# Slot experts reordered: layer one of all experts first, weights fetched in another order, one direct block instead of two

## The chip, the cores and the metric

The kernel runs on one core of a Trainium2 chip. The metric is the device time of one execution in microseconds (us), lower is better. Five queues of instructions run beside each other on the core: TensorE (PE in the rows; matmuls, and PEld for the loads of their stationary operand), VectorE (DVE), ScalarE (ACT), GpSimd (POOL) and SyncE (SP), which here only issues transfers (DMA).

## The reference

Three parts follow each other; the change touches the end of the second and the start of the third.

```python
# 1: attention with decay, 4 batches x 8 heads, 576 positions, head size 64 -> x of (2304, 512)
# 2: soft mixture of 8 experts with 4 slots each
logits = x @ phi                                  # (2304, 32)
d = softmax(logits, axis=0); slot_input = (d.T @ x).reshape(8, 4, 512)
for e in range(8):                                # "slot experts"
    h = np.maximum(slot_input[e] @ w1[e], 0.0)    # layer one: 512 -> 1024
    slot_out[e] = h @ w2[e]                       # layer two: 1024 -> 512
x = softmax(logits, axis=1) @ slot_out.reshape(32, 512)
# 3: dense mixture of 4 experts
for e in range(4):
    h = np.maximum(x @ m1[e], 0.0)                # m1: 512 x 1024
    out += p[:, e:e + 1] * (h @ m2[e])            # m2: 1024 x 512
```

## The kernel before, in words

**Weights.** All expert weights come as tiles of 128 x 1024 floats (512 KB), four for a layer of an expert, through `load_w` (L60), which takes the next one of the list `stream` and issues it on SP's queue. The order of the list is w1 and w2 of expert 0, of expert 1, and so on, then m1 and m2 of the dense experts. Tiles go, in this order, into `ring` (one buffer of four tiles), `ringb` (29 buffers), three pairs that take the place of attention's operands (`load_pair`), five tiles in `post`, issued when attention's buffers are free, and four in `post2`, issued when the tail of the slot soft-max is through with its space. That makes 48 tiles. The rest is loaded into buffers that the slot experts release (the dictionary `later`): w1 of expert six into `ring`, then w2 of six, w1 and w2 of seven and m1 of dense expert 0 into `ringb`, and m2 of dense expert 0 into `ring` as the last.

**Slot experts** (L746 to L830 and the first half of the block behind L948). `layer1(e)` multiplies all 32 slots with w1 of expert e: 32 matmuls with 32 stationary columns and 256 moving ones, four of them side by side in the array, into a PSUM bank; ScalarE takes the positive part. `turn(e)` transposes the result in two matmuls, GpSimd clears the tile `ht`, and VectorE copies the four slots that belong to the expert into it. `layer2(e)` is 16 matmuls of 512 moving columns, which add up in `so_ps` over all experts. TensorE runs layer one of the next expert between turn and layer two. A helper `c4_rep` on GpSimd makes replicas of the combine weights, which TensorE transposes (`c4_tr`) and ScalarE copies (`c4_hi`). `g_make` multiplies the slot outputs with m1, `g_spread` brings that into the layout of the gates `gs`, and `pieces` makes the hidden layer of a block of 256 rows: four matmuls for each half.

**Dense part.** Four experts x nine blocks of 256 rows. A *direct* block multiplies the hidden layer's quarters with the four quarters B00, B10, B01, B11 of m2, each split in a high (rounded) and a low part (`w_hi` on ScalarE, `w_lo` on VectorE or GpSimd): 8 products, 96 matmuls of 256 columns. Any other block needs 7 products, 84 matmuls, with sums T1 to T4 of the quarters (`w_sum`, GpSimd, 128 x 512 at a time), also split in two parts, and sums S1 to S4 of the hidden layer. Low parts of S1 to S4 are made by GpSimd in the block itself (L922). Before, the first two blocks are direct (`ND = 2`), and the quarters and sums of dense expert 0 are split while these run (`PRE0`). TensorE also makes the pieces of the block behind in each block (8 matmuls).

**Order.** Where `manual_schedule` names an engine, its instructions stand in program order; elsewhere a planner orders them. Before, the slot experts name TensorE only, the passage to the dense part names TensorE, ScalarE and VectorE, and the dense part all four. SP's queue is ordered by the planner. A pool of buffers that is opened over the space of closed ones waits for the instructions that use those.

Of the kernel before, what the change touches and what calls it, by code (L numbers as in the profile page):

```python
# [19 lines left out]
DM = H * D  # L20
# [14 lines left out]
def soft_moe_kernel(tc, a, out):  # L35
# [10 lines left out]
    NB = 29  # L46
    ND = 2
    with ExitStack() as top:
# [3 lines left out]
        ringb = attn.enter_context(tc.tile_pool(name="ringb", bufs=NB))  # L52
# [10 lines left out]
        def load_w(pl, n=1):  # L63
            for _ in range(n):
                kind, e, p = stream.pop(0)
# [7 lines left out]
        def load_ring():  # L73
            t = ring.tile([128, 4096], F32, tag="w", name=f"ring_{len(stream)}")
            for i in range(4):
                load_w(t[:, 1024 * i:1024 * i + 1024])
            return t
# [42 lines left out]
        def load_q(pr, r=slice(0, 128)):  # L120
            t = ringb.tile([128, 1024], F32, tag="w", name="q_1")[:, 0:S] if pr == 1 else raw[:, 0]
            sp.dma_start(out=t[r], in_=a["q"][pr, r])
            q_raw[pr] = t
# [26 lines left out]
        si_t = tl.tile([128, DC, 32], F32, name="si_t")  # L150
# [12 lines left out]
        pool.memset(mm[:, 0:1], -1e30)  # L163

# [343 lines left out]
        pre = ["ring"] * 4 + [ringb] * NB  # L508
        rt = []
        order = ExitStack()  # L510
        for g in range(NG + 4):
            pr, st = divmod(g, NS)
            if g < NG:
# [18 lines left out]
                if pre and g >= GW and g % PS == PO:  # L532
                    pl = pre.pop(0)
                    if pl == "ring":
                        if not rt:
                            rt.append(ring.tile([128, 4096], F32, tag="w", name="ring_0"))
                        pl = rt[0][:, 4096 - 1024 * (len(pre) - NB + 1):4096 - 1024 * (len(pre) - NB)]
# [13 lines left out]
        load_w(ex.enter_context(tc.tile_pool(name="post", bufs=5)), 5)  # L551
# [13 lines left out]
        with tc.manual_schedule(engines={E.PE, E.Activation, E.DVE}):  # L565
# [89 lines left out]
            for h in range(2):  # L655
                c = slice(2 * h, 2 * h + 2)
                dve.tensor_tensor(si_t[:, c], so[:, c], si_ps[h], op=ALU.add)
# [22 lines left out]
        def c4_rep(b):  # L680
            src = cn[:64, :, 4] if b == B else cn[:, b, 0:4]
            r = src.shape[0]
            c4 = c4p.tile([r, 4, 4, 32], F32, tag="c4f" if b == B else "c4", bufs=1 if b == B else 2, name=f"c4_{b}")
            chi = c4p.tile([r, 4, 32], F32R, tag="chi", name=f"chi_{b}")
# [60 lines left out]
        hrs = {}  # L745

        def layer1(e):
            t = ops.tile([128, DM], F32, tag="o", name="first") if e == 1 else bank(1, e % 2)
            w1 = wt["w1", e]
            for c in range(DC):  # L750
                for jq in range(4):
                    pe.matmul(t[32 * jq:32 * jq + 32, 0:256], lhsT=si_t[:, c, :],
                              rhs=w1[c][:, 256 * jq:256 * jq + 256], start=c == 0, stop=c == DC - 1)
            t = t[:, 0:256]
            hrs[e] = eo.tile([128, 256], F32, tag="hr", name=f"hr_{e}")
            act.activation(hrs[e], t, AF.Relu)

        hts = {}

        def turn(e):  # L760
            t = bank(0, e % 2)
            t = t[:, 0:256].rearrange("p (i q) -> p i q", i=2)
            for i in range(2):
                pe.transpose(t[:, i, :], hrs[e][:, 128 * i:128 * i + 128], ident)
# [26 lines left out]
        raws[0] = None  # L791
        later = {0: (ring, 4), 1: (ringb, 8), 2: (ringb, len(stream) - 44), 3: (ringb, 4), 5: (ring, 4)}
        layer1(0)
        for e in range(E1 - 2):
            with tc.manual_schedule(engines={E.PE}):
                if e == 0:
                    layer1(1)
                    turn(0)
                    layer1(2)
                    layer2(0)  # L800
                elif e == 1:
                    turn(1)
                    layer2(1)
                else:
                    turn(e)
                    layer1(e + 1)
                    layer2(e)
            if e in later:
                if later[e][0] is ring:
                    raws[0] = load_ring()  # L810
                else:
                    load_w(*later[e])
            if e == 5:
                ex.close()
                wsp = [top.enter_context(tc.tile_pool(name="wspa", bufs=1, side="right"))]
                c4tp = top.enter_context(tc.tile_pool(name="c4tp", bufs=1, side="right"))
                c4t = c4tp.tile([128, NT], F32R, name="c4t")
                so_t = c4tp.tile([128, DC, 32], F32, name="so_t")
                dpn = c4tp.tile([128, 18, E2], F32, name="dpn")
                sel = c4tp.tile([128, 4, 2, 128], F32R, name="sel")  # L820
                dpr = c4tp.tile([128, 18, E2], F32, name="dpr")
                dps = c4tp.tile([128, 18], F32, name="dps")
                sp.dma_start(out=dpr, in_=a["dp"])
                gsp = top.enter_context(tc.tile_pool(name="gsp", bufs=2, side="right"))
                cq = ExitStack()
                c4p = cq.enter_context(tc.tile_pool(name="c4p", bufs=1, side="right"))
                pool.memset(f32(sel), 0.0)
                for jq in range(4):
                    for i in range(2):
                        r = slice(32 * jq, 32 * jq + 32)  # L830
                        pool.tensor_scalar(sel[r, jq, i, 64 * i:64 * i + 64].rearrange("p (a s) -> p a s", a=2),
                                           i4[r, None, :].to_broadcast([32, 2, 32]), 1.0, 1.0, op0=ALU.mult,
                                           op1=ALU.mult)
                for b in (B, 0, 1):
                    c4_rep(b)
# [107 lines left out]
        with tc.manual_schedule(engines={E.PE, E.Activation, E.DVE}):  # L943
            turn(E1 - 2)
            layer1(E1 - 1)
            layer2(E1 - 2)
            turn(E1 - 1)
            c4_tr(B, c4_bank(B))  # L948
            c4_tr(0, c4_bank(0))
            for h in range(2):  # L950
                act.copy(orow[h], so_ps[:, 256 * h:256 * h + 256])
            free += [0, 1, 2, 3]
            c4_hi(B)
            c4_hi(0)
            for h in range(2):
                layer2_last(h)
            w_hi(0, "B00", act, 0, 2)
            c4_rep(2)
            for h in range(2):
                t = (bank(1, 1) if h == 0 else c4_bank("so"))[:, 0:64].rearrange("p (c s) -> p c s", c=2)  # L960
                for c in range(2):
                    pe.matmul(t[:, c, :], lhsT=orow[h][:, 128 * c:128 * c + 128], rhs=i4)
                dve.tensor_copy(so_t[:, 2 * h:2 * h + 2], t)
                if h == 0:
                    c4_tr(1, c4_bank(1))
                    c4_hi(1)
            c4_rep(3)
            w_lo(0, "B00", pool, 0, 2)
            w_hi(0, "B00", act, 2, 4)
            g_make(0, bank(0, 0)[:, 0:256], range(2))  # L970
            gg = g_make(0, bank(0, 0)[:, 0:256], range(2, DC))
            c4_tr(2, c4_bank(2))
            c4_hi(2)
            c4_tr(3, c4_bank(3))
            c4_hi(3)
            cq.close()
            attn.close()
            accp = top.enter_context(tc.tile_pool(name="accp", bufs=1))
            wsp.append(top.enter_context(tc.tile_pool(name="wspb", bufs=1)))
            top.enter_context(tc.tile_pool(name="skew", bufs=1)).tile([128, 24], F32, name="skew")  # L980
            hp = top.enter_context(tc.tile_pool(name="hp", bufs=1))
            ttp = top.enter_context(tc.tile_pool(name="ttp", bufs=1))
            free += [4, 5, 6, 7]
            for hf in range(2):
                g_spread(0, *gg, hf)
            pieces(0, 0)
            hi_d(0, 0, 0)
            lo_d(0, 0, 0)
            w_hi(0, "B10", act, 0, 2)
            w_lo(0, "B10", pool, 0, 2)  # L990
            hi_d(0, 0, 1)
            lo_d(0, 0, 1)
            pieces(0, 1)
            hi_d(0, 1, 0)
            lo_d(0, 1, 0)
            w_lo(0, "B00", dve, 2, 4)
            w_hi(0, "B10", act, 2, 4)
            w_lo(0, "B10", pool, 2, 4)
# [261 lines left out]
```

## Time and profile before

| | |
|---|---|
| median of 3 runs | 660.17 us (660.02 to 660.5) |
| profiled execution | 661.34 us, of it 659.5 in the span of the trace |
| TensorE busy | 649.1 us (98%) |
| VectorE, ScalarE, GpSimd busy | 486.6 (74%), 349.1 (53%), 417.3 (63%) |
| moved by DMA | 76.15 MB |

Attention runs to 201, the tail of the slot soft-max to 210, the slot experts to 244, the passage to 251, the dense part from there to the end. A busy share is an average over these stages; what ends last is read in each stage by itself. Times in rows are from the start of the span.

### The profile page before, as it was taken

The page shows a single profiled execution, that of the slowest core. Times are in us where ns is not written, and L with a number is a line of the kernel's source. Part 1 is how long each engine was busy: PE and PEld are TensorE (multiplying, and loading weights), DVE is VectorE, ACT ScalarE, POOL GpSimd, SP SyncE. Part 2 cuts the span into 40 slices and gives each one's busy share as a digit, 9 for nine tenths or more (in the row PEclk, how much of TensorE's full clock was granted, in tenths as well). Part 3 has the DMA queues.
Part 4 walks back from the last instruction along what each step waited for, and adds up shares of the span by engine and source line. Part 5 has one row for each costly group of instructions (what it writes and reads, how often), then busy time and mean ns, then how long its engine had stood idle before and what let it go on. Part 6 is the DMA issues. An engine that isn't in the chain of part 4 may idle for free.

```text
span 659.5 us, 15363 instructions
## 1 busy us (share of the span) xinstructions
PE 649.1 (98%) x5670; PEld 579.9 (88%) x5670; DVE 486.6 (74%) x1322; ACT 349.1 (53%) x844; POOL 417.3 (63%) x398
## 2 busy tenths in 40 slices
PE   8999999999999999999999999999999999999998
PEld 4778788788787448999999999999999999999997
DVE  6889889888884017777678877678877768876774
ACT  6777877777772025633457433538343446444441
POOL 5677777777641068833989653789753689844443
PEclk9999999999999999999999999999999999999999
DMA  5687687775347990303000303000303000011111
GB/s 170 192 241 224 210 263 225 221 247 167 86 167 268 411 419 27 127 3 128 1 1 1 129 1 129 1 1 1 129 1 129 2 1 1 33 49 49 58 40 65
DMA packets 27509, 76.15 MB, mean 115 GB/s; under 512 B 4014, under 2 KB 4654, under 8 KB 27436
## 3 DMA queue, kind: packets, MB, share of 16 engines
q1 hardware_dynamic: 27436, 75.18, 33.8%
q8 instruction: 45, 0.74, 0.5%
q14 instruction: 28, 0.23, 0.1%
HBM read 70.31 MB, written 4.72 MB: 114 GB/s over the span
## 4 chain that ended last, share of the span: by engine, by line
PE 86%; DMA 4%; DVE 3%; ACT 3%; issue 2%; POOL 0%; ACTq 0%; DVEq 0%
PE R L1049 27%; PE Q L1049 13%; PE P L1049 7%; PE avb L283 5%; PE pt L266 5%; PE two L856 5%; PE d L1069 3%; PE sc L233 3%; PE sc L217 3%; PE sc L230 3%; PE pl L335 2%; PE ava L295 2%; PE pt L257 2%; DMA w<-in_w 2%; DMA ring<-in_m 1%
## 5 line engine op out<-in xcount | busy, mean ns | idle before, releaser
L922 POOL TENSOR_TENSOR s<-S,s 128x512 fp32r<-128x512 f32 x136 | 174.8, 1317 | 134.4 <-ACT s L918 134.4
L918 ACT CAST s<-S 128x512 fp32r<-128x512 f32 x136 | 75.0, 619 | 86.0 <-PE Q L1049 49.5
L207 ACT ACTIVATE p<-p,nm 128x256 f32<-128x256 f32 (+2 forms) x144 | 83.4, 579 | 28.8 <-DVE nm L203 27.5
L1049 PE MATMUL R<-wh_T,s 128*128 128x256 f32 x544 | 86.5, 280 | 0.7 <-DVE acc L1032 0.7
L1032 DVE SCALAR_TENSOR_TENSOR acc<-R,dpn,acc 128x256 f32<-128x256 f32 x115 | 55.5, 482 | 36.8 <-PE R L1049 33.6
L888 ACT ACTIVATE a<-two 128x256 f32<-128x256 f32 x68 | 26.0, 383 | 96.4 <-PE two L856 96.0
L1049 PEld LDWEIGHTS R<-wh_T,s 128*128 128x128 f32 x544 | 73.6, 188 | 1.5 <-ACT a L897 1.3
L203 DVE CUSTOM_DVE_ANT_0 p<-sc,maskb 128x256 f32<-128x256 f32 (+2 forms) x144 | 66.9, 489 | 3.3 <-PE sc L217 1.1
L914 DVE SCALAR_TENSOR_TENSOR S<-two,S 128x256 f32<-128x256 f32 x136 | 57.1, 420 | 3.3 <-POOL s L922 0.5
L914 DVE SCALAR_TENSOR_TENSOR S<-two,a 128x256 f32<-128x256 f32 x136 | 56.4, 414 | 0.0
L184 POOL TENSOR_TENSOR opd<-raw,opd 64x576 fp32r<-64x576 f32 x29 | 42.4, 1461 | 14.0 <-ACT opd L169 12.9
L266 PE MATMUL pt<-ident,p 128*128 128x128 f32 x285 | 45.9, 279 | 1.3 <-ACT p L207 0.7
L856 PE MATMUL two<-c4t,gs 128*128 128x256 f32 x288 | 46.2, 283 | 0.9 <-ACT gs L169 0.9
L230 PE MATMUL sc<-opd 128*128 128x256 f32 (+3 forms) x128 | 46.5, 374 | 0.0
L904 DVE SCALAR_TENSOR_TENSOR q<-two,q 128x512 fp32r<-128x512 f32 x68 | 46.3, 681 | 0.0
L266 PEld LDWEIGHTS pt<-ident,p 128*128 128x128 f32 x285 | 31.4, 140 | 14.6 <-issue 10.2
L1049 PE MATMUL R<-wh_T,q 128*128 128x256 f32 x272 | 43.6, 282 | 0.0
L192 POOL TENSOR_TENSOR opd<-raw,opd 64x576 fp32r<-64x576 f32 x30 | 42.3, 1409 | 1.4
L1049 PE MATMUL R<-wh_B,a 128*128 128x256 f32 x272 | 43.0, 280 | 0.0
L1049 PE MATMUL P<-wh_B,q 128*128 128x256 f32 x272 | 43.0, 279 | 0.0
L1049 PE MATMUL Q<-wh_T,s 128*128 128x256 f32 x272 | 43.0, 280 | 0.0
L1049 PE MATMUL Q<-wh_B,s 128*128 128x256 f32 x272 | 43.0, 280 | 0.0
(272 smaller groups left out, 1658.0 us busy)
## 6 DMA issues: line engine op xcount, KB each, us to landing
w<-in_w SPq DMA_DIRECT2D x50, 512.0 KB
ring<-in_m SPq DMA_DIRECT2D x28, 512.0 KB
raw<-in_k SPq DMA_DIRECT2D x64, 144.0 KB
v<-in_v SPq DMA_DIRECT2D x16, 320.0 KB
out<-acc SPq DMA_DIRECT2D x17, 256.0 KB
ring<-in_w SPq DMA_DIRECT2D x8, 512.0 KB
raw<-in_q SPq DMA_DIRECT2D x28, 144.0 KB
w_opd<-in_w SPq DMA_DIRECT2D x4, 512.0 KB
```

What stands on the lines that cost most here:

```text
L184: (dve if h == 0 else pool).tensor_tensor(lo, r, f32(hi), op=ALU.subtract)
L203: dve.tensor_tensor_reduce(out=pt_in[j][:, k0:k0 + n], in0=sc, in1=maskb[:, m0:m0 + n], scale=-SCALE, scalar=nm, op0=ALU.add, op1=ALU.min, ...
L207: act.activation(p, p, AF.Exp, bias=nm, scale=-1.0, accum_out=sums)
L230: pe.matmul(o, lhsT=qa[hh][:, qs], rhs=ka[hh][:, 0:n], start=True, stop=False)
L266: pe.transpose(t[:, i, :], pt_in[j][:, 128 * i:128 * i + 128], ident)
L856: pe.matmul(t[:, j, k], lhsT=gs[e][:, 128 * fc:128 * fc + 128], rhs=c4t[:, nb * BLK:nb * BLK + BLK])
L904: dve.scalar_tensor_tensor(o[:, 1], i, 0.0, f32(o[:, 0]), op0=ALU.max, op1=ALU.subtract)
L914: dve.scalar_tensor_tensor(sv[m, name][:, c], half[m, h][:, :, k, 128 * t:128 * t + 128], 0.0, other, op0=ALU.max, op1=op)
L918: act.copy(tile_of(m, name)[:, 0], sv[m, name])
L922: (eng or pool).tensor_tensor(o[:, 1], sv[m, name], f32(o[:, 0]), op=ALU.subtract)
L1032: dve.scalar_tensor_tensor(o, t, pcol, o, op0=ALU.mult, op1=ALU.add)
L1049: pe.matmul(t, lhsT=a[:, c, :], rhs=w[:, c, :], start=first and x == 0 and c == 0, stop=x == 2 and c == 3, skip_group_check=True)
```

## The change

- `stream` lists w1 of all experts, then w2 of all, then m1 and m2. `ringb` becomes two pools of 17 and 14 buffers, the second of which is given up early (`brief`); `post` takes six tiles. 51 tiles are fetched ahead. The first four behind them are m2 of dense expert 0, into `ring`; then the last 13 of w2, then m1 of dense expert 0.
- The slot inputs lie in `si_f`, with 28 zero columns about the four of an expert, so that `layer1` of four experts adds up in one bank. ScalarE and `turn` run once for four experts; `slots(e)` makes an expert's `ht` with one multiply by a mask (`own`) on VectorE, in place of GpSimd's memset and the copy.
- The order is layer one of all eight, then layer two of all eight, with all four engines in program order from there to the end.
- Copies, sums and low parts of m2's quarters are placed among the last slot experts, and T1 and T2 get space there; one direct block is left (`ND = 1`), and `PRE0` holds only the rest.
- The scratch for dynamic DMA goes from its default size to 1024 bytes, and three memsets stand at the start.

```diff
-    NB = 29
-    ND = 2
+    NB = (17, 14)
+    ND = 1
...
-        ringb = attn.enter_context(tc.tile_pool(name="ringb", bufs=NB))
+        ringb = [attn.enter_context(tc.tile_pool(name="ringb", bufs=NB[0]))]
+        brief = ExitStack()
+        ringb.append(brief.enter_context(tc.tile_pool(name="ringc", bufs=NB[1])))
...
-        stream = [(kind, e, p) for e in range(E1) for kind in ("w1", "w2") for p in range(4)]
+        stream = [(kind, e, p) for kind in ("w1", "w2") for e in range(E1) for p in range(4)]
...
+        pool.memset(own, 0.0)
+        pool.memset(own.rearrange("p (e x) -> p e x", x=36)[:, :, 0:4], 1.0)
+        pool.memset(si_f, 0.0)
...
-        pre = ["ring"] * 4 + [ringb] * NB
+        pre = ["ring"] * 4 + [ringb[0]] * NB[0] + [ringb[1]] * NB[1]
...
-        load_w(ex.enter_context(tc.tile_pool(name="post", bufs=5)), 5)
+        load_w(ex.enter_context(tc.tile_pool(name="post", bufs=6)), 6)
...
         def layer1(e):
-            t = ops.tile([128, DM], F32, tag="o", name="first") if e == 1 else bank(1, e % 2)
+            t = l1[e // 4]
             w1 = wt["w1", e]
             for c in range(DC):
+                o = 128 * e + 32 * c
                 for jq in range(4):
...
+                    pe.matmul(t[32 * jq:32 * jq + 32, :], lhsT=si_f[:, o:o + 32],
+                              rhs=w1[c][:, 256 * jq:256 * jq + 256], start=e % 4 == 0 and c == 0,
+                              stop=e % 4 == 3 and c == DC - 1)
...
+        def slots(e):
             ht = eo.tile([128, 2, 4, 32], F32, tag="ht", name=f"ht_{e}")
-            pool.memset(ht, 0.0)
-            dve.tensor_copy(ht[:, :, :, 4 * e:4 * e + 4],
-                            t.rearrange("p a (j s) -> p a j s", j=4)[:, :, :, 4 * e:4 * e + 4])
+            dve.tensor_tensor(ht, tr1[e // 4],
+                              own[:, None, None, 32 * e:32 * e + 32].to_broadcast([128, 2, 4, 32]), op=ALU.mult)
...
+        man.enter_context(tc.manual_schedule(engines={E.PE, E.Activation, E.DVE, E.Pool}))
+        for e in range(E1):
+            if e == 4:
+                hidden(0)
+            layer1(e)
+            if e == 0:
+                raws[0] = load_ring(stream.index(("m2", 0, 0)))
+            elif e < 6:
+                load_w(ringb[0], 4 if e < 5 else 1)
+            if e == 4:
+                turn(0)
+                slots(0)
+                slots(1)
+        hidden(1)
+        for e in range(5):
+            layer2(e)
+            if e == 0:
+                turn(1)
+            if e < 3:
+                slots(e + 2)
+        ex.close()
+        brief.close()
...
+        for x in ("T1", "T2"):
+            w_sum(0, x, 0, 2)
+            w_sum(0, x, 2, 4)
+        pool.memset(f32(sel), 0.0)
...
+        w_hi(0, "B00", act)
+        w_hi(0, "B10", act)
+        w_lo(0, "B00", dve, 0, 2)
+        slots(5)
+        layer2(5)
+        w_hi(0, "B01", act)
+        w_hi(0, "B11", act)
+        w_hi(0, "T2", act)
+        w_hi(0, "T1", act)
+        for b in (0, 1, 2, 3, B):
+            c4_rep(b)
+        w_lo(0, "B00", dve, 2, 4)
+        slots(6)
+        w_lo(0, "B10", dve, 0, 2)
+        slots(7)
+        w_lo(0, "B10", dve, 2, 4)
...
+        g_make(0, bank(0, 0)[:, 0:256], range(2))
+        gg = g_make(0, bank(0, 0)[:, 0:256], range(2, DC))
+        for b in (1, 2):
+            c4_tr(b, c4_bank(b))
+            c4_hi(b)
+        for x in ("B01", "B11"):
+            w_lo(0, x, pool, 0, 2)
+            w_lo(0, x, pool, 2, 4)
+        for x in ("T3", "T4"):
+            w_sum(0, x, 0, 2)
+            w_sum(0, x, 2, 4)
...
+        PRE0 = {(0, 0): [("lo", "T2", "p", 0, 2)], (0, 1): [("hi", "T3", "a", 0, 4), ("lo", "T2", "p", 2, 4)],
+                (0, 2): [("hi", "T4", "a", 0, 4), ("lo", "T1", "p", 0, 2)], (0, 3): [("lo", "T1", "p", 2, 4)],
+                (0, 4): [("lo", "T3", "p", 0, 2)], (0, 5): [("lo", "T3", "p", 2, 4)],
+                (0, 6): [("lo", "T4", "p", 0, 2)], (1, 0): [("lo", "T4", "p", 2, 4)]}
...
-    nc = bacc.Bacc("TRN2", target_bir_lowering=False, num_devices=1)
+    nc = bacc.Bacc("TRN2", target_bir_lowering=False, num_devices=1, dynamic_dma_scratch_size=1024)
```

## Rows read from the trace of the kernel before

**Rows 1.** The chain that ended last, 224 to 262: start, length, what.

```profile
224.68 0.37 PE two L764 x2
225.05 1.86 PE two L752 x32
226.92 1.72 PE so_ps L776 x16
...
238.64 8.15 DMA ring<-in_m
```

**Rows 2.** Busy time of each engine by stretch, granted clock, DMA share, GB/s.

```profile
160.00:170.00 10.00, 10.00 (x94) 7.75 (x94) 8.67 (x35) 7.95 (x26) 7.96 (x9) 1.00 0.28 76
...
209.00:212.00 3.00, 2.94 (x40) 2.17 (x44) 1.25 (x7) 0.14 (x1) 1.02 (x3) 1.00 0.02 5
...
214.00:246.00 32.00, 31.65 (x396) 14.44 (x396) 2.83 (x12) 4.31 (x11) 11.31 (x30) 1.00 1.02 414
...
248.00:250.00 2.00, 1.16 (x8) 0.96 (x8) 0.69 (x1) 2.00 (x5) 1.89 (x2) 1.00 0.25 89
...
656.40:659.50 3.10, 0.00 (x0) 0.00 (x0) 0.46 (x1) 0.00 (x0) 0.00 (x0) 0.93 0.32 118
```

**Rows 3.** SP's timeline, 209 to 243: first issue, time to the last, what, count.

```profile
211.09 1.75 SPq L71 DMA_DIRECT2D w<-in_w  x4
...
212.93 1.89 SPq L71 DMA_DIRECT2D ring<-in_w  x4
214.92 15.32 SPq L71 DMA_DIRECT2D w<-in_w  x12
231.32 4.00 SPq L71 DMA_DIRECT2D m<-in_m  x4
236.21 3.97 SPq L71 DMA_DIRECT2D ring<-in_m  x4
```

**Rows 4.** Waits of SP's queue, 150 to 260: total, times, longest.

```profile
SPq L71 <- POOL cn L660: 1.1, 1, 1.1
```

**Rows 5.** Timeline of TensorE and ScalarE, 209 to 278 (idle before, releaser).

```profile
210.48 1.93 PE L752 MATMUL two<-ring,si_t 128*32 128x256 f32 x32
...
245.01 1.93 PE L928 MATMUL two<-m,so_t 128*32 128x256 f32 x32
...
246.79 0.62 ACT L737 CAST wh_B<-ring 128x512 fp32r<-128x512 f32 x1 [4.34 <-DMA ring<-in_m]
...
246.88 1.09 PE L694 MATMUL ct<-ident,c 128*128 128x128 f32 x8
...
247.88 0.62 ACT L737 CAST wh_B<-ring 128x512 fp32r<-128x512 f32 x1
...
251.50 0.39 PE L1069 MATMUL d<-wh_B,q 128*128 128x256 f32 x1 [0.21 <-ACT q L863]
...
276.88 0.63 PE L1049 MATMUL R<-wh_B,a 128*128 128x256 f32 x4
```

**Rows 6.** The chain in the dense part: a stretch of direct matmuls, two starts of blocks.

```profile
271.39 5.66 PE d L1069 x48
...
580.13 2.12 PE R L1049 x18
...
590.95 2.12 PE R L1049 x18
```

**Rows 7.** Groups by shape: count, busy us, mean ns of one, idle before.

```profile
L724 POOL TENSOR_TENSOR T<-ring 128x512 f32<-128x512 f32 x8 | 10.3, 1306 | 2.1 <-DMA ring<-in_m 2.1
...
L737 ACT CAST wh_B<-ring 128x1024 fp32r<-128x1024 f32 x9 | 9.4, 1049 | 0.0
...
L743 DVE TENSOR_TENSOR wl_B<-ring,wh_B 128x512 fp32r<-128x512 f32 x3 | 4.6, 1549 | 0.0
```

**Rows 8.** GpSimd's timeline: at the start, and the selector's memset.

```profile
4.91 0.77 POOL L182 TENSOR_SCALAR opd<-raw 64x576 fp32r<-64x576 f32 x1 [1.42 <-DMA raw<-in_q]
...
232.91 0.95 POOL L827 MEMSET sel<- 128x1024 f32 x1
```

More of the change, by code (lines that the diff above doesn't have):

```diff
@@ L120, in load_q @@
         def load_q(pr, r=slice(0, 128)):
[L121 removed]
+            t = ringb[1].tile([128, 1024], F32, tag="w", name="q_1")[:, 0:S] if pr == 1 else raw[:, 0]
             sp.dma_start(out=t[r], in_=a["q"][pr, r])
@@ L149, in soft_moe_kernel @@
         s_sb = tl.tile([128, DM], F32, name="s_sb")
-        si_t = tl.tile([128, DC, 32], F32, name="si_t")
+        si_f = tl.tile([128, E1 * 132], F32, name="si_f")
+        own = tl.tile([128, E1 * 36], F32, name="own")
+        si_t = si_f.rearrange("p (e x) -> p e x", x=132)[:, :, 0:128].rearrange("p e (c y) -> p e c y", y=32)[:, :, :, 0:4]
         mm = tl.tile([128, 5], F32, name="mm")
@@ L743, in w_lo, with hidden, turn @@
             eng.tensor_tensor(lo[:, c0:c1], source(e, name)[:, c0:c1], f32(hi[:, c0:c1]), op=ALU.subtract)
[L745 removed]
+        hrs, tr1, hts = {}, {}, {}
         def layer1(e):
[L748 removed]
+            t = l1[e // 4]
             w1 = wt["w1", e]
             for c in range(DC):
+                o = 128 * e + 32 * c
                 for jq in range(4):
[L752 to L762, printed above, removed]
+                    pe.matmul(t[32 * jq:32 * jq + 32, :], lhsT=si_f[:, o:o + 32],
+                              rhs=w1[c][:, 256 * jq:256 * jq + 256], start=e % 4 == 0 and c == 0,
+                              stop=e % 4 == 3 and c == DC - 1)
+        def hidden(g):
+            hrs[g] = eo.tile([128, 256], F32, tag="hr", name=f"hr_{g}")
+            act.activation(hrs[g], l1[g], AF.Relu)
+        def turn(g):
+            t = bank(g, 0)[:, 0:256].rearrange("p (i q) -> p i q", i=2)
             for i in range(2):
[L764 removed]
+                pe.transpose(t[:, i, :], hrs[g][:, 128 * i:128 * i + 128], ident)
+            tr1[g] = t.rearrange("p a (j s) -> p a j s", j=4)
+        def slots(e):
             ht = eo.tile([128, 2, 4, 32], F32, tag="ht", name=f"ht_{e}")
[L766 to L768 removed]
+            dve.tensor_tensor(ht, tr1[e // 4],
+                              own[:, None, None, 32 * e:32 * e + 32].to_broadcast([128, 2, 4, 32]), op=ALU.mult)
             hts[e] = ht
@@ L790, in soft_moe_kernel @@
         so_ps = ops.tile([128, DM], F32, tag="o", name="so_ps")
[L791 to L835, printed above, removed]
@@ new lines, in soft_moe_kernel @@
+        l1 = [bank(1, 0)[:, 0:256], ops.tile([128, DM], F32, tag="o", name="first")[:, 0:256]]
+        man = ExitStack()
+        man.enter_context(tc.manual_schedule(engines={E.PE, E.Activation, E.DVE, E.Pool}))
[11 more added lines that the diff above has]
+                slots(1)
@@ new lines, in soft_moe_kernel @@
+        hidden(1)
[7 more added lines that the diff above has]
+        brief.close()
+        wspa = top.enter_context(tc.tile_pool(name="wspa", bufs=1, side="right"))
+        c4tp = top.enter_context(tc.tile_pool(name="c4tp", bufs=1, side="right"))
+        c4t = c4tp.tile([128, NT], F32R, name="c4t")
+        so_t = c4tp.tile([128, DC, 32], F32, name="so_t")
+        dpn = c4tp.tile([128, 18, E2], F32, name="dpn")
@@ new lines, in soft_moe_kernel @@
+        sel = c4tp.tile([128, 4, 2, 128], F32R, name="sel")
+        dpr = c4tp.tile([128, 18, E2], F32, name="dpr")
+        dps = c4tp.tile([128, 18], F32, name="dps")
+        sp.dma_start(out=dpr, in_=a["dp"])
+        gsp = top.enter_context(tc.tile_pool(name="gsp", bufs=2, side="right"))
+        wsp = [top.enter_context(tc.tile_pool(name="wspb", bufs=1, side="right")), wspa]
+        ttp = top.enter_context(tc.tile_pool(name="ttp", bufs=1, side="right"))
+        cq = ExitStack()
+        c4p = cq.enter_context(tc.tile_pool(name="c4p", bufs=1, side="right"))
@@ new lines, in soft_moe_kernel @@
+        free += range(8)
+        for x in ("T1", "T2"):
+            w_sum(0, x, 0, 2)
+            w_sum(0, x, 2, 4)
+        pool.memset(f32(sel), 0.0)
+        for jq in range(4):
+            for i in range(2):
+                r = slice(32 * jq, 32 * jq + 32)
+                pool.tensor_scalar(sel[r, jq, i, 64 * i:64 * i + 64].rearrange("p (a s) -> p a s", a=2),
+                                   i4[r, None, :].to_broadcast([32, 2, 32]), 1.0, 1.0, op0=ALU.mult,
+                                   op1=ALU.mult)
@@ L941, in c4_bank @@
             return ops.tile([128, DM], F32, tag="o", name=f"ct_{b}")
[L943 to L998, printed above, removed]
-            hi_d(0, 1, 1)
-            lo_d(0, 1, 1)
-            w_hi(0, "B01", act, 0, 2)
-            w_lo(0, "B01", pool, 0, 2)
-            w_hi(0, "B01", act, 2, 4)
-            w_lo(0, "B01", dve, 2, 4)
-            w_hi(0, "B11", act, 0, 2)
-            w_lo(0, "B11", pool, 0, 2)
-            w_hi(0, "B11", act, 2, 4)
-            w_lo(0, "B11", dve, 2, 4)
-            dve.tensor_reduce(dps, dpr, axis=AX.X, op=ALU.add)
-            dve.tensor_scalar(dps, dps, 1e-9, None, op0=ALU.add)
-            dve.reciprocal(dps, dps)
-            dve.tensor_tensor(dpn, dpr, dps[:, :, None].to_broadcast([128, 18, E2]), op=ALU.mult)
@@ new lines, in soft_moe_kernel @@
+        layer2(E1 - 2)
+        for h in range(2):
+            act.copy(orow[h], so_ps[:, 256 * h:256 * h + 256])
+        for h in range(2):
+            layer2_last(h)
+        for h in range(2):
+            t = (bank(1, 1) if h == 0 else c4_bank("so"))[:, 0:64].rearrange("p (c s) -> p c s", c=2)
+            for c in range(2):
+                pe.matmul(t[:, c, :], lhsT=orow[h][:, 128 * c:128 * c + 128], rhs=i4)
+            dve.tensor_copy(so_t[:, 2 * h:2 * h + 2], t)
+            if h == 0:
+                c4_tr(0, c4_bank(0))
+                c4_hi(0)
@@ new lines, in soft_moe_kernel @@
+        g_make(0, bank(0, 0)[:, 0:256], range(2))
[9 more added lines that the diff above has]
+            w_sum(0, x, 2, 4)
+        attn.close()
+        accp = top.enter_context(tc.tile_pool(name="accp", bufs=1))
+        top.enter_context(tc.tile_pool(name="skew", bufs=1)).tile([128, 24], F32, name="skew")
@@ new lines, in soft_moe_kernel @@
+        hp = top.enter_context(tc.tile_pool(name="hp", bufs=1))
+        for hf in range(2):
+            g_spread(0, *gg, hf)
+        c4_tr(3, c4_bank(3))
+        pieces(0, 0)
+        hi_d(0, 0, 0)
+        lo_d(0, 0, 0)
+        hi_d(0, 0, 1)
+        lo_d(0, 0, 1)
+        c4_tr(B, c4_bank(B))
+        pieces(0, 1)
+        hi_d(0, 1, 0)
+        lo_d(0, 1, 0)
+        hi_d(0, 1, 1)
+        lo_d(0, 1, 1)
+        c4_hi(3)
+        c4_hi(B)
+        cq.close()
+        dve.tensor_reduce(dps, dpr, axis=AX.X, op=ALU.add)
@@ L1112, in soft_moe_kernel @@
         g_next = {}
-        with tc.manual_schedule(engines={E.PE, E.Activation, E.DVE, E.Pool}):
+        with man:
             for m in range(NM):
```

22 lines of the change are left out of this document (13 added, 9 removed), and 5 rows, old and new, of the table PRE0.

## Prediction, before the result was known

> **What bounds the kernel now.** I read four views in this order: the chain that ended last, the transfers, the timeline around the slot experts, and the groups of costs. TensorE is busy 98% of the span, so a gain can only come from matmuls that disappear or from the few places where it waits. The chain is on TensorE nearly everywhere; in the slot experts it leaves it. There an expert is a layer one (1.86 us), a layer two (1.72) and a turn (0.37), 3.95 together, and then the chain goes into transfers, the last of them 8.15 us long and ending at 246.8 [rows 1]. The reader is to see that the stage is a stream: from 214 to 246 the DMA engines are busy throughout at 414 GB/s, after standing still from 209 to 212 [rows 2]. A tile of 512 KB takes 0.524/0.414 = 1.27 us. The stream begins at 211.1, when the queue's wait for the last instruction of the soft-max tail (cn) ends [rows 3, 4], and holds 28 tiles: 4 of the second group behind the tail, 4 into the ring, 12 for experts six and seven, 4 of m1 and 4 of m2 [rows 3]. So the tile whose arrival ScalarE shows at 246.79, the first of m2, is the 25th [rows 5]. TensorE itself ended m1's product at 246.88; then copies of the m2 weights and of the gates share ScalarE, and the dense part starts at 251.50, with short waits in its first two blocks [rows 5]. From 276.88 on, the blocks of seven products follow each other in 10.82 us [rows 5, 6].
>
> **The change part by part.**
>
> Three tiles move ahead of the stream: two into the attention stage, where the DMA engines are busy 28% between 160 and 170, and one into the group behind the attention, whose transfer falls into the idle 209 to 212 [rows 2]. I take nothing for the first two, hidden by idle engines; if they delayed a transfer that attention waits for, the bound is one tile, 1.27 us. So 25 tiles are left behind 211.1. But their order changes too: m2 now goes into the ring as tiles 5 to 8, and m1 comes last. The last tile of m1 is the 25th, and by its place it lands when the 25th lands now: 246.8. The slot experts' last weight tile is the 21st, 4 x 1.27 earlier, 241.7.
>
> TensorE in the slot experts: layer ones and twos stay, eight turns become two. Without waits: 210.48 + 8 x (1.86 + 1.72) + 2 x 0.37 = 239.9 [rows 1, 5], 6 x 0.37 = 2.2 less than with eight turns. These are not gained: the last expert waits for 241.7, and the product with m1 for 246.8. Its last quarter then takes 1.93/4, about 0.4 [rows 5], so it ends at 247.2, 0.3 later than now. Six turns less are thus worth nothing, the stream covers them; if the stream were a tile faster, they would be worth 1.3. The masked multiply on VectorE that replaces a memset and a small copy has no row of its own; between an empty instruction (nothing) and the dearest 128x512 of VectorE (1.55 us [rows 7]) I take about 0.5, and one is due in each 1.7 of layer two, so it hides even at the upper bound.
>
> From the product with m1 to the first direct matmul it is 251.50 - 246.88 = 4.62 us now. In it, ScalarE's second half of B00 (247.88, 0.62) stands ahead of the gates' copies [rows 5]. The change does all copies of m2's weights before. ScalarE does them (six of 1.05 [rows 7]) from about 231, when layer two of expert two has released the space of their tiles (210.48 + 14.9 + 0.37 + 3 x 1.72 = 230.9), to 237.5, ahead of the copies of the slot output, which are due at 238 or later. With 0.5 to 0.6 out of the path and the 0.21 that the first matmul waited for ScalarE gone, I take 3.8 us: start of the dense part at 251.0, **-0.5**. Bounds: a tile later or earlier in the stream, -1.8 to +0.8.
>
> The first two blocks: 251.50 to 276.88 is 25.38 us for 192 direct matmuls and 16 of the pieces for the blocks behind; at 5.66/48 = 0.118 each [rows 6] that is 24.53. The 0.85 us of waits are for halves of B00 and B10 that VectorE and GpSimd subtract while the block runs. In the change these are subtracted before. **-0.85**, bounds -0.85 and 0.
>
> One direct block becomes seven products: 104 x 0.1179 = 12.26 against 10.82 [rows 6]: **-1.44**. This needs T1 to T4 split in time, which is GpSimd's work. Its list, now in program order: four sums, then the selector and five replicas of the combine weights, four low halves, four sums, seven low halves, and only then the low part of S2 of the first block of seven products. A 128x512 of it takes 1.31 [rows 7]. The sums can start when layer two of expert zero releases their space (227.4; m2 landed at 225). 227.4 + 5.2 = 232.6; the selector and the replicas are bounded by all that GpSimd does from 214 to 246 now, 11.3 [rows 2]: 243.9; 8 x 1.31: 254.4; 7 x 1.31: 263.6; S2: 264.9. The block begins at 251.0 + 12.3 = 263.3 and wants S2's low part after two products, four pieces and two thirds of the third, 1.41 + 0.47 + 1.41 + 0.94 later (a product is 12 matmuls), at 267.5. S1, two instructions behind it, is there at 267.5 and wanted a product later, at 268.9. So 1.4 us are to spare, and there is no term.
>
> At the start three memsets more stand on GpSimd's queue, some 1,400 columns. The nearest rows are its other memsets; the gap in front of them is 1.42 us, until q arrives at 4.91 [rows 8], about what they need at the 0.95 us per 1,024 columns that the selector's memset takes [rows 8]. Nothing, bound +0.8 if they slow VectorE's first instructions beside them. The smaller scratch only moves addresses: nothing.
>
> Sum: -0.5 - 0.85 - 1.44 = -2.8 us. The profiled execution took 661.34 (span 659.5 and 1.84 around it): 658.5. The runs' median is 1.17 below it: 657.4.
>
> **The rivals.** *GpSimd's list starts late (slower).* If its first sum waits for more than its own space, up to the release of the prefetched weights behind layer two of expert four (210.48 + 14.9 + 0.37 + 5 x 1.72 = 234.4), the whole list is 7.0 later, 5.6 beyond the 1.4 that S1 has to spare: 663.0. It turns the sign from a first sum at about 231.6 on, 1.4 + 2.8 behind the time that I take. For it: one queue in program order, and space of several pools overlaid. Against: the sums' tiles lie, by the sizes in the code, over layer-one weights alone.
>
> *GpSimd and VectorE slow each other.* The trace has VectorE's 128x512 subtraction at 1.55 [rows 7]. If GpSimd's 19 large instructions before S2 were 0.2 longer, the list would be 3.8 late, 2.4 beyond its slack: 659.8.
>
> [...]
>
> *The stream is not the bound (faster still).* If the 25 tiles run without the gap of the present stream or start earlier, m1 is there a tile sooner: 657.4 - 1.3 = 656.1. Even TensorE alone would end the slot experts at 239.9.
>
> **How the numbers follow.** The forecast has 0.62 (656.0 to 658.7, its own bounds but the extreme ones); the faster stream 0.08; the two engines in each other's way 0.10; the clock 0.06; the late list 0.14. The range leaves out the late list and the far end of the faster stream: 655.8 to 660.6. A difference of 0.2% (1.3 us) is what a measurement can tell from none. Faster by more: the forecast and the faster stream, 0.70. Within: the two engines in each other's way and the clock, 0.16. Slower: the late list, 0.14.
>
> **What would show it.** Right: ScalarE's copies of m2's weights all before 240; the product with m1 waiting for a transfer and ending near 247.2; the first direct matmul near 251.0; no TensorE wait for a low half; the first block of seven products some 12.3 later; from there on 10.8 a block. Wrong: a first sum on GpSimd after 232, a TensorE wait for GpSimd in the second block, a granted clock under 1 between 240 and 260, a later end of the attention, or a stream that begins at another time than 211.

## The result and the profile after

665.78 us (median of 4 runs, 664.76 to 666.66) against 660.33 for the kernel before on the same chip: a ratio of 1.0083, interval 1.0063 to 1.0102. The change made the kernel slower by 5.4 us where 2.8 less were forecast, and the time lies outside the range. The profiled execution has a span of 664.9, against 659.5 before, also 5.4 more; its rows say where they arise. (The profiled execution after is the slowest of its four, the one before lies 1.2 us above its median.)

The first thing to read is where the slot experts begin. The chain that ended last, 212 to 269 (start, length, what):

```profile
212.12 7.11 PE two L762 x128
...
228.18 9.48 DMA w<-in_w
237.73 9.92 DMA m<-in_m
247.69 0.64 PE two L959 x8
...
256.39 8.81 DVE dps L1020
...
266.79 0.75 DVE S L945 x2
...
268.08 1.62 PE R L1059 x6
```

Layer one starts at 212.12, not 210.48 [rows 5]: 1.64 us are lost before the changed stage begins. Inside the stage the chain is in the transfers, as forecast. SP's timeline shows the new order, m2 into the ring first and m1 last; its wait for cn is 1.1 as before [rows 3, 4]:

```profile
214.59 1.95 SPq L73 DMA_DIRECT2D ring<-in_m  x4
...
234.04 4.02 SPq L73 DMA_DIRECT2D m<-in_m  x4
```

TensorE's timeline from there on (start, busy, what; idle before and its releaser):

```profile
247.69 0.64 PE L959 MATMUL two<-m,so_t 128*32 128x256 f32 x8 [0.51 <-DMA m<-in_m]
...
252.46 0.28 PE L1079 MATMUL d<-wh_B,q 128*128 128x256 f32 x1
...
268.08 1.19 PE L1059 MATMUL R<-wh_B,a 128*128 128x256 f32 x4 [3.12 <-DVE acc L1040]
...
281.67 0.51 PE L1059 MATMUL R<-wh_B,a 128*128 128x256 f32 x3
```

From layer one to the first direct matmul it is 252.46 - 212.12 = 40.34, before 41.02 [rows 5]: 0.68 less. The direct block should then end at 252.46 + 12.26 = 264.72, but the first product starts at 268.08, 3.36 later, and the block of seven products behind it takes 281.67 - 268.08 = 13.59 in place of 10.82 [rows 6], 2.77 more. The engines behind TensorE's wait, VectorE and then GpSimd:

```profile
256.14 0.22 DVE L1019 TENSOR_REDUCE dps<-dpr 128x18 f32<-128x72 f32 x1
256.39 8.79 DVE L1020 TENSOR_SCALAR dps<-dps 128x18 f32<-128x18 f32 x1
```
```profile
229.81 2.52 POOL L733 TENSOR_TENSOR T<-ring 128x512 f32<-128x512 f32 x2 [17.11 <-PE so_ps L787]
...
253.88 2.54 POOL L733 TENSOR_TENSOR ring<-ring,T 128x512 f32<-128x512 f32 x2
256.39 5.03 POOL L752 TENSOR_TENSOR wl_T<-T,wh_T 128x512 fp32r<-128x512 f32 x4
261.38 3.77 POOL L752 TENSOR_TENSOR wl_T<-ring,wh_T 128x512 fp32r<-128x512 f32 x3
```

The reader is to see two ends that agree: an addition over 18 columns lasts from 256.39 to 265.18, and GpSimd's list, which runs without a gap, ends at 265.15. `dpn` is the weight with which VectorE takes each result out of PSUM (`acc`), so those takes, and the sums S, queue up behind it, and TensorE finds no free bank: its wait of 3.12 at 268.08 ends with a take. The clock follows, in the windows (span; busy of PE, PEld, DVE, ACT, POOL; granted clock; DMA share, GB/s):

```profile
11.00:18.00 7.00, 6.72 (x28) 5.76 (x27) 4.84 (x19) 4.55 (x14) 5.69 (x6) 0.52 0.53 147
...
264.70:268.00 3.30, 0.26 (x3) 0.06 (x1) 3.20 (x10) 0.00 (x0) 0.45 (x1) 0.89 0.00 0
268.00:274.00 6.00, 5.92 (x28) 5.95 (x29) 4.44 (x11) 3.22 (x7) 3.48 (x3) 0.50 0.01 3
```

TensorE works for 0.26 of the 3.3 us to 268, and from 268 to 274 the granted clock is 0.50. At the start it was low too, 0.52 in the mean from 11 to 18, after TensorE had stood for 1.58 ahead of its first scores at 8.99.

The balance: 1.64 - 0.68 = 0.96 up to the first direct matmul; 281.67 - 252.46 = 29.21 against 25.38 [rows 5] for the first two blocks, 3.83 more, which is the 3.36 + 2.77 lost against the forecast's prices, less the 0.85 + 1.44 that these had as gains; and 0.6 in all blocks behind, many of which take 10.86 instead of 10.82 [rows 6]:

```profile
585.24 2.12 PE R L1059 x18
...
596.10 2.12 PE R L1059 x18
```

Sum 5.4. The start of the span holds the cause of the 1.64. The first rows of VectorE in the kernel before, then of VectorE and of GpSimd after:

```profile
3.76 0.52 DVE L487 TENSOR_SCALAR fr<-fr 64x256 f32<-64x256 f32 x2 [3.76 <-DMA fr<-in_f]
```
```profile
3.47 1.64 DVE L494 TENSOR_SCALAR fr<-fr 64x256 f32<-64x256 f32 x2 [3.47 <-DMA fr<-in_f]
```
```profile
3.42 0.35 POOL L168 MEMSET own<- 128x288 f32 x1
3.69 0.99 POOL L170 MEMSET si_f<- 128x1056 f32 x1
4.61 0.13 POOL L169 MEMSET own<- 128x32 f32 x1
```

The same pattern: two clips on VectorE take 1.64 in place of 0.52 while GpSimd's three fills run from 3.42 to 4.74. They end 0.83 later, and TensorE's first scores come 0.80 later, before and after:

```profile
8.19 0.69 PE L230 MATMUL sc<-opd 128*128 128x256 f32 x1
```
```profile
8.99 0.35 PE L237 MATMUL sc<-opd 128*128 128x256 f32 x1 [1.58 <-ACT opd L509]
```

The rest of the 1.64 arises behind them; the stretch at 0.52 lies there.

### The profile page after: what moved, and what is told of

The parts are those of the page before. It is cut to its first block, busy times and chain, and to the rows that moved or that the text cites. A ratio compares the mean times of both kernels' runs of the same rounds, so it can differ in the third digit from the quotient of the medians.

```text
span 664.9 us, 15324 instructions
## 1 busy us (share of the span) xinstructions
PE 651.0 (98%) x5646; PEld 583.4 (88%) x5646; DVE 495.5 (75%) x1332; ACT 348.8 (52%) x840; POOL 424.0 (64%) x402
## 4 chain that ended last, share of the span: by engine, by line
PE 86%; DVE 6%; DMA 4%; ACT 2%; issue 2%; DVEq 0%; ACTq 0%; SPq 0%
PE R L1059 28%; PE Q L1059 14%; PE P L1059 7%; PE pt L273 5%; PE avb L290 5%; PE two L887 5%; PE sc L240 3%; PE sc L237 3%; PE sc L224 3%; PE pl L342 2%; PE ava L302 2%; PE pt L264 2%; DMA m<-in_m 1%; DMA w<-in_w 1%; DVE dps L1020 1%
## 5 line engine op out<-in xcount | busy, mean ns | idle before, releaser
L953 POOL TENSOR_TENSOR s<-S,s 128x512 fp32r<-128x512 f32 x140 | 179.8, 1318 | 141.7 <-ACT s L949 141.7
L949 ACT CAST s<-S 128x512 fp32r<-128x512 f32 x140 | 77.1, 619 | 96.0 <-PE Q L1059 52.0
L1059 PE MATMUL R<-wh_T,s 128*128 128x256 f32 x560 | 89.2, 281 | 0.6 <-DVE acc L1042 0.6
L1059 PEld LDWEIGHTS R<-wh_T,s 128*128 128x128 f32 x560 | 75.9, 188 | 1.4 <-ACT a L928 1.1
L945 DVE SCALAR_TENSOR_TENSOR S<-two,S 128x256 f32<-128x256 f32 x140 | 58.9, 420 | 3.6 <-POOL s L953 1.1
L945 DVE SCALAR_TENSOR_TENSOR S<-two,a 128x256 f32<-128x256 f32 x140 | 58.1, 415 | 0.0
L191 POOL TENSOR_TENSOR opd<-raw,opd 64x576 fp32r<-64x576 f32 x29 | 42.6, 1468 | 14.4 <-ACT opd L176 13.3
L1059 PE MATMUL R<-wh_B,a 128*128 128x256 f32 x280 | 45.3, 284 | 3.1 <-DVE acc L1040 3.1
L1059 PE MATMUL P<-wh_B,q 128*128 128x256 f32 x280 | 45.1, 283 | 0.0
L1059 PE MATMUL R<-wl_T,s 128*128 128x256 f32 x280 | 44.3, 280 | 0.0
```

The lines of the kernel that those rows point to most:

```text
L191: (dve if h == 0 else pool).tensor_tensor(lo, r, f32(hi), op=ALU.subtract)
L945: dve.scalar_tensor_tensor(sv[m, name][:, c], half[m, h][:, :, k, 128 * t:128 * t + 128], 0.0, other, op0=ALU.max, op1=op)
L949: act.copy(tile_of(m, name)[:, 0], sv[m, name])
L953: (eng or pool).tensor_tensor(o[:, 1], sv[m, name], f32(o[:, 0]), op=ALU.subtract)
L1059: pe.matmul(t, lhsT=a[:, c, :], rhs=w[:, c, :], start=first and x == 0 and c == 0, stop=x == 2 and c == 3, skip_group_check=True)
```

## Experiments

The theory after the result (it turned out too wide, see below): an instruction of VectorE can be kept out as long as GpSimd issues without a gap; at the start the fills do it, in the direct block the low halves. Rivals: the form of the one addition; moved addresses; the clock alone. All runs are of the changed kernel with an edit, except where the kernel before is named.

**Form or gap.** `e1_two_inputs` changes the form, `e2_memsets_late` writes the fills behind the attention in the program, `e3_both` does both, `e4_gpsimd_waits` gives GpSimd a reason to pause.

```diff
-        dve.tensor_scalar(dps, dps, 1e-9, None, op0=ALU.add)
+        dve.scalar_tensor_tensor(dps, dps, 1e-9, dps, op0=ALU.add, op1=ALU.max)   # e1, e3
...
         avs.close()
+        pool.memset(own, 0.0)                                                     # e2, e3
...
-        dve.tensor_tensor(dpn, dpr, dps[:, :, None].to_broadcast([128, 18, E2]), op=ALU.mult)
+        pool.tensor_tensor(dpn, dpr, dps[:, :, None].to_broadcast([128, 18, E2]), op=ALU.mult)   # e4
```

> The changed kernel, with one VectorE instruction in another form: the addition of 1e-9 to the 128x18 sums of the probabilities (8.8 us in the changed kernel) has two SBUF inputs instead of one and a constant. Theory (VectorE's copy-like instruction with one SBUF input is shut out for as long as GpSimd runs one large instruction after another): it takes under 1.5 us, TensorE does not wait for it, the clock stays up from 250 on, and the time falls by the 3.4 us of the wait and the 2.9 us of the half clock, to 659.5. Rival (TensorE really waits for GpSimd's list, and the long instruction only stands beside it): the wait of 3 us stays under another name, time over 663.

> The changed kernel, with the three new memsets at the end of the attention instead of the start. Theory (they shut out VectorE's first instruction in the same way): that instruction takes 0.3 instead of 1.4 us, attention is 1.6 to 1.7 us earlier throughout, time 664.1. Rival (the start is later because of the smaller scratch and the moved addresses): attention stays where it is, 665.8.

> Both edits, two inputs and late memsets, together. Theory: the two add up, 657.5 to 658, so the sum of the prediction's own terms comes out. Rival (something else in the new order holds TensorE as soon as these two are gone): between 659 and 661.

> The changed kernel; the last of the four small instructions on the probabilities (their product with the reciprocal, 128x72) goes to GpSimd, in front of its seven low halves, so that GpSimd has to wait for VectorE there. The 128x18 addition keeps its form. Theory (only the missing gap on GpSimd counts): the addition takes under 0.6 us, time 659.5 to 660. Rival (that form is slow at this place by itself, whatever GpSimd does): it stays near 8.8 us and the time over 665.

e1: 665.62, ratio 1.0075 (1.006 to 1.009), the addition at 8.87 us. The form with two inputs is kept out just as long, so my theory of the one form fell. e2: 665.65, 1.0076 (1.0061 to 1.0092), and e3: 666.45, 1.009 (1.0075 to 1.0105). They tell nothing of late fills: the planner, which orders GpSimd there, put the fills back to 3.42, as e2's trace shows:

```profile
3.69 0.99 POOL L558 MEMSET si_f<- 128x1056 f32 x1
```

e4: 663.43, 1.0048 (1.0032 to 1.0065). GpSimd stands for 0.41 us, and the addition takes 0.22:

```profile
255.74 0.22 DVE L1020 TENSOR_SCALAR dps<-dps 128x18 f32<-128x18 f32 x1
```
```profile
256.34 0.32 POOL L1022 TENSOR_TENSOR dpn<-dpr,dps 128x72 f32<-128x72 f32 x1 [0.41 <-DVE dps L1021]
256.62 5.07 POOL L752 TENSOR_TENSOR wl_T<-T,wh_T 128x512 fp32r<-128x512 f32 x4
```

TensorE's 3 us wait and the low clock behind it are gone (four matmuls into R take 0.64 at 264.11, in the changed kernel 1.19 at 268.08), so at this place a pause of GpSimd ends VectorE's wait. The time misses the 659.5 to 660 that were expected. The four runs lie between 660.7 and 664.3, and only the run at 660.7 has a trace; its mean granted clock was 0.997, that of the others 0.991 to 0.994, so they ran longer at a lower clock, and where is not known.

**The start.** The fills are worked out from a value of the eleventh pair of heads, so that they can't stand early (`e5_late`); with e4's edit (`e6_late_gap`); the fills alone in the kernel before, into a ring tile that is not yet in use (`e7_before_memsets`); the scratch alone there (`e8_before_scratch`).

```diff
...
-        pool.memset(si_f, 0.0)
...
             rinv[pr] = ri
+            if pr == 10:
+                zero = ri[:, 0, 0:1]
...
+                pool.tensor_scalar(si_f, zero.to_broadcast([128, E1 * 132]), 0.0, 0.0, op0=ALU.mult, op1=ALU.add)
```

> The changed kernel whose three fills of own and si_f are worked out from a denominator of the eleventh pair of heads (times 0, plus 0 or 1), so that they cannot stand at the start. In all five traces with the fills at the start, VectorE's first instruction ends at 4.9 us, with the fills, instead of near 4.1. Theory (the fills hold VectorE, and with it the whole attention, late): first transposes of the probabilities back from 29.83 to 28.1 to 28.4, time 665.8 - 1.5 = 664.3; the 8.8 us addition at the direct blocks and PE's wait of 3 us stay. Rival (the later start comes from moved addresses or from the clock): the start stays at 29.3 or later and the time at 665.5 or more.

> The fills late as in the run before, and the multiplication of dpn on GpSimd, ahead of its seven low halves, so that GpSimd pauses while VectorE sums dps. Theory (two separate losses, the start and the shut-out with the clock's fall behind it): 665.8 - 1.6 - 6.3 = 657.9, range 657 to 659, so faster than before by about 2.5 us, as the forecast's own sum had it. Rival (one loss only hides another that waits behind it, for example weights of the stream): 660 or more, with a new wait of TensorE in the first direct blocks.

> The kernel before with three fills of the same sizes at the same place in GpSimd's list, into a tile that nothing uses then. Theory (the fills alone cost the start): VectorE's first instruction ends near 4.9 instead of 4.05, first transposes at 29.3 to 30 instead of 28.09, time 660.4 + 1.2 to 2 = 661.6 to 662.4. Rival (start set by something else in the change): 660.4, first transposes at 28.1.

> The kernel before with the smaller scratch of the DMA lists alone (all tiles of the left side move by 15360 bytes). If the 10.86 instead of 10.82 us of the later blocks comes from addresses: about 660.8, blocks of 10.86. If not: 660.4, blocks of 10.82.

e5: 664.03, 1.0057 (1.0041 to 1.0072). The clips are back at 0.52, and the first matmuls into pl (the first transposes of the expectations, which count them 0.17 earlier than the timeline does) stand at 28.02 against 30.00 in the changed kernel and 28.26 before; the addition still takes 9.04. How much of the late start is the clock's can be read beside e1, where it did not fall there (a matmul into sc of 128x384 takes 0.34 at 11.35, in the changed kernel 0.48 at 11.21): in e1 the first scores are 0.95 later than before and the first matmuls into pl 1.21, in the changed kernel, at 0.52, they are 0.80 and 1.74 later. e7: 662.26, 1.0036 (1.0021 to 1.0051), so the fills alone cost the kernel before 2.4 us (1.4 to 3.4). Its clips:

```profile
3.61 1.40 DVE L491 TENSOR_SCALAR fr<-fr 64x256 f32<-64x256 f32 x2 [3.61 <-DMA fr<-in_f]
```

In its trace the first matmuls into pl come at 28.86, 0.6 later than before, with a clock of 1.00 in the first 20 us; its ten runs reach from 661.4 to 665.0, so the price differs by execution, and what the slower ones lose more is not shown. e8: 660.37, 0.9997 (0.9987 to 1.0007), blocks still 10.82: the scratch is free, as forecast.

e6: 659.38, 0.9984 (0.9974 to 0.9993), faster than both kernels. It was expected at 657.9 (657 to 659), so it stays short by about a microsecond and a half, and the rows show where. TensorE, then GpSimd and VectorE in it:

```profile
250.20 0.28 PE L1081 MATMUL d<-wh_B,q 128*128 128x256 f32 x1
...
262.54 0.64 PE L1061 MATMUL R<-wh_B,a 128*128 128x256 f32 x4
...
271.13 0.70 PE L1061 MATMUL Q<-wh_B,s 128*128 128x256 f32 x4 [0.38 <-DVE acc L1042]
...
274.02 0.64 PE L1061 MATMUL R<-wh_B,a 128*128 128x256 f32 x4
```
```profile
266.34 3.79 POOL L955 TENSOR_TENSOR s<-S,s 128x512 fp32r<-128x512 f32 x3
```
```profile
270.17 0.42 DVE L947 SCALAR_TENSOR_TENSOR S<-two,S 128x256 f32<-128x256 f32 x1 [0.56 <-POOL s L955]
```

The direct block takes 12.34, the first block of products 11.48 in place of 10.82. What is late there is GpSimd's list: a sum S of the next block waits until GpSimd has read the old one, and the take that frees the bank for the sixth product (271.13) stands behind that sum in VectorE's queue.

**What is left, and what bounds it.** Two direct blocks in e6 (`e9_fixed_nd2`, ND = 2), the spacer tile moved (`e10_fixed_skew`, 24 to 280 floats), the stream four tiles shorter (`e11_fixed_stream`: the eighth slot expert's second layer is not loaded and uses the seventh one's weights, so its output is another), and, in the changed kernel itself, two other forms (`e12_forms`).

```diff
-        stream = [(kind, e, p) for kind in ("w1", "w2") for e in range(E1) for p in range(4)]
+        stream = [(kind, e, p) for kind in ("w1", "w2") for e in range(E1) for p in range(4)][:-4]   # e11
...
-            dve.tensor_scalar(lf[:, n], lf[:, n], 1e-4, 1.0, op0=ALU.max, op1=ALU.min)
+            dve.tensor_reduce(lf[:, n], lf[:, n][:, :, None], axis=AX.X, op=ALU.max)                 # e12
...
-        dve.tensor_scalar(dps, dps, 1e-9, None, op0=ALU.add)
+        dve.tensor_reduce(dps, dps[:, :, None], axis=AX.X, op=ALU.max)                               # e12
```

> The kernel with both losses mended (fills late, GpSimd pausing), but with two direct blocks as in the kernel before. Forecast's own price for the second direct block: 12.26 - 10.82 = 1.44. If that is what the block is worth, 659.4 + 1.44 = 660.8, less 0.4 to 0.6 if GpSimd's list, which has 11 us more, no longer holds the first block of products: 660.2 to 660.8. Rival (the second direct block was free, since GpSimd's list holds the products that take its place): 659.4.

> The mended kernel with the spacer tile of the dense part 280 instead of 24 floats, so that the accumulators behind it move by 1024 bytes. If the 10.85 to 10.87 us of the blocks (10.82 before) comes from where these tiles lie: blocks of 10.82 and 658.9. If not: the same 10.86 and 659.4.

> The mended kernel with four tiles less in the stream: the second layer of the eighth slot expert uses the seventh one's weights, and its own are not loaded. Theory (the start of the dense part is set by the stream: m1's last tile is its 25th, 1.3 us a tile): the product with m1 and the first direct matmul come 4 to 5 us earlier, near 245.5 instead of 250.1; of that GpSimd's list of low halves, which does not get earlier, takes part back in the first blocks: 655.5 to 658. Rival (ScalarE, GpSimd or the layer-two chain sets the start): first direct matmul at 249.5 or later, 659 or more.

> The changed kernel with nothing moved, but two instructions of VectorE in another form: the clip of f at the start and the addition of 1e-9 to dps are each a tensor_reduce over one element (the clip and the 1e-9 are left out). [...] Rival (any instruction of VectorE with all operands in SBUF is shut out): the reduces themselves take 0.8 us longer and 8.8 us, and the time stays at 665.8.

e9: 660.39, 0.9999 (0.999 to 1.0009), 1.0 above e6 on ratios 0.0015 apart. The intervals overlap a little, so the size is uncertain; it fits what the rows give, that the second direct block is worth 1.5 less the 0.66 that GpSimd's list takes back.

e10: 659.43, 0.9986 (0.9977 to 0.9995), blocks of 10.86 as in e6. Moving the accumulators by 1024 bytes does not remove the 0.04 a block; its cause stays open.

e11: 659.49, 0.998 (0.9971 to 0.9989). The product with m1 starts at 240.38 instead of 245.43 and the first direct matmul at 246.43 instead of 250.20: the stream does set the start. But nothing arrives at the end:

```profile
246.43 0.28 PE L1081 MATMUL d<-wh_B,q 128*128 128x256 f32 x1
...
265.44 0.74 PE L1061 MATMUL R<-wh_T,s 128*128 128x256 f32 x4 [2.26 <-POOL s L955]
...
271.35 0.71 PE L1061 MATMUL Q<-wh_B,s 128*128 128x256 f32 x4 [0.38 <-DVE acc L1042]
```

GpSimd's list ends where it did, and TensorE waits for it: the 3.8 us are given back. The start moved as the theory said, but GpSimd took back all of it and not a part. The addition is kept out once more, beside a shorter rest of the list:

```profile
250.37 4.35 DVE L1022 TENSOR_SCALAR dps<-dps 128x18 f32<-128x18 f32 x1
```

It starts 4.3 us before GpSimd's pause at 254.7 and ends there.

e12: 663.69, 1.0043 (1.0026 to 1.006), somewhat under the 664.3 to 665.2 that were expected if the wait passes from the addition to the multiplication. Here the form decides which of the small instructions is kept out:

```profile
255.38 0.17 DVE L1020 TENSOR_REDUCE dps<-dps 128x18 f32<-128x18 f32 x1
...
255.88 7.92 DVE L1022 TENSOR_TENSOR dpn<-dpr,dps 128x72 f32<-128x72 f32 x1
```

The addition as a reduce runs beside GpSimd in 0.17, and the multiplication with two inputs in SBUF takes the wait over, to the end of GpSimd's list at 263.7. At the start the two reduces take 0.81 us together beside the same fills, and the first matmuls into pl come at 28.50 instead of 30.00. If each waited only for the instruction of GpSimd that was running, the wait would be at most one low half of GpSimd, 1.26 us (5.03 for four); the rows show 4.35, 7.92 and 8.8 us, in each case until GpSimd's queue paused.

**Where VectorE does get its turn.** A list without a gap is not enough for these long waits. In the kernel before, the same addition and the same multiplication ran beside such a list, and each waited only for the end of one instruction of GpSimd, at 260.29 and 261.5:

```profile
259.79 0.53 DVE L1010 TENSOR_SCALAR dps<-dps 128x18 f32<-128x18 f32 x1
...
260.65 0.97 DVE L1012 TENSOR_TENSOR dpn<-dpr,dps 128x72 f32<-128x72 f32 x1
```
```profile
258.55 1.74 POOL L743 TENSOR_TENSOR wl_B<-ring,wh_B 128x512 fp32r<-128x512 f32 x1
260.24 1.29 POOL L724 TENSOR_TENSOR ring<-ring 128x512 f32<-128x512 f32 x1
```

In the changed kernel a subtraction of VectorE (two inputs in SBUF) got in between two sums of GpSimd that follow each other without a gap; it ended at 234.12, and GpSimd's second sum took 1.74 instead of 1.29:

```profile
232.83 1.29 DVE L752 TENSOR_TENSOR wl_B<-ring,wh_B 128x512 fp32r<-128x512 f32 x1
```
```profile
232.28 2.98 POOL L733 TENSOR_TENSOR T<-T,ring 128x512 f32<-128x512 f32 x2
```

So the long wait is shown for the small addition and multiplication at this place of the changed kernel, and that a pause of GpSimd ends it; what decides whether VectorE gets its turn behind one instruction of GpSimd is open. It is not the form or the size of VectorE's instruction alone, since the same two were let in before. The tiles' addresses and what ran on both engines just before were not varied by themselves.

## Why the prediction failed, step by step

- **Stream and m1: right.** The product with m1 waits for a transfer (247.69), the chain ends in m<-in_m, e11 moves the start by moving the stream. ScalarE's copies of m2's weights lie at 231.5 to 237.8, all before 240. First sum on GpSimd at 229.81, earlier than the 231.6 from which the rival would have decided.
- **Start of the dense part, -0.5: right.** -0.68 from layer one on. The two signs of being wrong that came true point elsewhere: the attention ends later, and the stream begins at 212.7 instead of 211.1, later by the same 1.64.
- **Waits of the first two blocks, -0.85, and the direct block, -1.44: right in size, hidden in the changed kernel.** With both losses mended, two direct blocks run without a wait (e9: 275.29 - 250.62 = 24.67, worked out as 24.53 in the forecast, so the waits were worth 0.71), and the one block in their place gives 12.34 + 11.48 = 23.82 in e6 against 25.38 before, -1.56; without the 0.66 that GpSimd's list takes, -2.2.
- **"There is no term" for GpSimd's list: wrong, twice.** The list was on time, but I priced only what waits for its results. What cost 3.36 is that it ran without a gap beside an addition that I had not priced at all, though VectorE's queue in the direct block hangs on it; the addition was kept out to the list's end, and TensorE's clock of 0.50 from 268 to 274, behind that stall, cost 2.77 more. And the 1.4 us to spare at S1 said nothing of the tiles that the list gives back: in e6 no product waits for a low part of S1 or S2, but the next block's sums wait for GpSimd, which costs 0.66.
- **"Nothing" for the three memsets: wrong.** I gave 0.8 as a bound, if they slowed VectorE's first instructions. They did: the clips took 1.1 longer, and the first scores came 0.80 later. The bound left out the clock, which was low (0.52 from 11 to 18) behind TensorE's wait of 1.58 for these scores; layer one came 1.64 later in the profiled execution, and the kernel before with these fills alone is 2.4 slower (1.4 to 3.4).
- **The rivals.** "GpSimd and VectorE slow each other" had the right pair and, where it cost time, the wrong direction: GpSimd's low halves kept their length (5.03/4 = 1.26), VectorE's addition did not. The clock's 0.06 is a term that no run shows: the changed kernel's clock was 1.00 from 240 to 260, and 0.50 from 268 to 274, behind the stall.
- **Not forecast:** 0.04 a block, 0.6 in all, which appears with the change and goes with neither the scratch (e8) nor the spacer (e10).

The failed step is therefore the pricing of GpSimd's list by its due times alone ("there is no term"): in its place the runs show 3.36 + 2.77 us in the direct block and the block behind it. The second one is "nothing" for the memsets: 1.64. The forecast's other terms hold, but that shows only with both losses mended. By the rows e6 has these gains (0.87 from layer one, at 210.05, to the first direct matmul; 0.71; 12.34 - 10.86 = 1.48) and loses 0.66 and 0.6 again, 1.8 in all; its measured gain is 1.1 us (0.5 to 1.7).

## What to carry to other kernels

When a list of GpSimd is made dense or moved, look at every instruction of VectorE that falls beside it and has its operands in SBUF alone: if it is in a form with two inputs or a tensor_scalar, price its wait as lasting to GpSimd's next pause, as it did for 128x18 and 128x72 (4.35 us in e11, 7.92 in e12, 8.79 in the changed kernel). In other places of these traces the wait was only one instruction of GpSimd (the same two took 0.53 and 0.97 in the kernel before); that is the lower end of the price, and the trace has to tell which it is. If something is queued behind it, let GpSimd itself take one step of that chain, so that it waits for VectorE once (e4: the addition took 0.22), or choose a reducing form (0.17 in e12), or an operand in PSUM (VectorE's sums and takes from PSUM kept 0.42 and 0.48 us beside the same list in e6). And check where a fill that is written late is really issued.

## What the runs showed that was not expected

- VectorE was passed over many times in a row: 128 x 18 floats took 8.8 us (seven instructions of GpSimd of 1.26 without a gap), 4.35 with a shorter rest, 0.22 with a pause of 0.41. The same addition took 0.53 in the kernel before, beside a list without a pause.
- 3.3 us in which TensorE did almost nothing were followed by six at a clock of 0.50 in the changed kernel; 2.2 us of waiting in e12 also brought a lower clock (0.72 in the mean from 266 to 272), and 2.26 in e11 did not (1.0 in the mean of the whole profiled execution).
